# Forgetting attention with a gated layer on one core: seven-product second layers moved from units 1-7 to units 2-8, weight sums cut into 16 pieces, transposes of results issued earlier

## The chip, the cores and the metric

The kernel runs on one core of one Trainium2 chip. The metric is the device time of the core in microseconds (us). A profile shows one execution; its span is the stretch from the first to the last recorded event, and its own time is a little longer than the span.

Engines are called as in the profile: PE (TensorE, matrix products), PEld (loading of PE's weights), DVE (VectorE), ACT (ScalarE), POOL (GpSimd) and SP (SyncE, here a queue of transfers).

## The reference

```python
batch, n_heads, seq, head_dim = (8, 8, 576, 64)      # q, k, v; f is (8, 8, 576)
d_model, d_ff = (512, 2048)

def _attn_ref(q, k, v, f):
    scores = scale * np.matmul(q, k.transpose(0, 1, 3, 2))
    cum = np.cumsum(np.log(np.clip(f, 0.0001, 1.0)), axis=-1)
    decay = cum[:, :, :, None] - cum[:, :, None, :]
    scores = np.where(causal, -1000000000.0, scores + decay)
    attn = np.exp(scores - np.max(scores, axis=-1, keepdims=True))
    attn = attn / (np.sum(attn, axis=-1, keepdims=True) + 1e-09)
    return np.matmul(attn, v)

x = attn_out.transpose(0, 2, 1, 3).reshape(4608, 512)
h = x @ w_in
out = (h - np.tanh(h)) @ w_out
```

So there is causal attention with a decay for 64 heads of 576 positions, and then two dense layers (512 to 2048 to 512) with a gate between them, on 4608 tokens.

## The kernel before, in words

**Attention** goes by pairs of heads: eight batches of four pairs, 32 pairs in all. A pair has seven score tiles (`scores`, `TILES`); each is two or so matmuls on PE, an exponential on ACT and, from batch 2 on, a mask on POOL. `values` multiplies the exponentials with v (30 small matmuls into `av`), and DVE norms the result into `xn`. `turn` then has SP transpose `xn` by two transfers into `XR`, a ring of three batches that holds the tokens as columns for the first layer. `values` and `turn` of a pair run in the slot of the following pair.

**The dense layers** go by nine units of 512 tokens (`UW`). `mlp1` is the first layer: 16 steps, each with four matmuls of 512 columns into a bank `hps`, a tanh on ACT and an addition on DVE (`gate`) which leaves a gated tile in 16 bits. The second layer has two forms:

- plain (`mlp2`): 16 steps of four matmuls of 512 columns.
- seven products (`seven`): the second layer is taken as a product of 2 x 2 blocks, and seven block products replace eight. A unit has 14 steps of eight matmuls of 256 columns (seven products, two halves `m` each). For this DVE forms four sums of the gated tile's quarters in each of four tiles (`sums`, L421), and once for the whole kernel sums of the second weight (`weight_sums`, L429): `t1`, `t2`, `t3`, `tn4`. They lie in the buffers that held q and k of batch 3 (`qn`, `kn` in the profile) and in `tn4`. The products gather in two banks, `cx` and `cz`; ACT copies `cx` out (L507, L515, L518, L523), DVE adds `cz` (L486), and four stores on SP (L483) write the result. Products 2 and 4 start `cz` afresh, products 3, 5 and 6 go on in `cx`.

`fast(u)` says which units use seven products: units 1 to 7. Units 0 and 8 are plain. The last block of rows of unit 8 is done by `last_rows` in two column parts.

**The order is written by hand** for all five engines. The list `mlp` holds all 274 steps of the dense layers in order. There are 33 slots of attention: those of the first batch are written out, and `slot(p, take)` runs from p = 4 to 32. It goes through the items of a pair (score tiles s0 to s6, turning of q and k for batches 1 and 2, `values`, `turn`, and the loads of `LOADS`) and puts `take` dense steps between them, evenly. `TAKE` has the counts. What is left of the steps, those of units 7 and 8, runs after the last slot: the tail, with no attention beside it.

`LOADS` hangs other work on a slot's score tile: loads of later batches (POOL), transposes of q and k (SP), their placing (`place`, L106, eight DVE copies in every fourth slot from p = 11 on) and the weight sums (p = 10).

Each engine does its instructions in the order in which they are written, and so does each queue of transfers. SP carries the transposes of `xn` and the stores of results in one queue.

The lines that fix a product's bank, and the sums that follow it:

```python
        ps = (x, x, z, z, x, x, z, z, x, x, x, x, z, z)[s]
        fresh = ph in (0, 1, 3)
```

Of the kernel before, what the change touches and what calls it, by code (L numbers as in the profile page):

```python
# [22 lines left out]
def kernel(  # L23
# [10 lines left out]
    nc = tc.nc  # L34
# [169 lines left out]
    def load_qk(dst, src, b, h0, h1):  # L204
# [3 lines left out]

    LOADS = {(NPAIR, 5): [lambda: load_qk(qn, q, 2, 0, H)],
             (NPAIR, 6): [lambda: load_qk(kn, k, 2, 0, H)]}  # L210
    for i, ti in enumerate((1, 2, 4, 5)):
        LOADS.setdefault((2 * NPAIR + 2, ti), []).append(lambda i=i: weight_sums(i))
    for b in range(2, B):
        p0 = (b - 1) * NPAIR
        for n in range(NJ):
# [191 lines left out]
        nc.vector.tensor_tensor(out=to, in0=view(hps), in1=view(th), op=ALU.add)  # L407

    def fast(u):
        return 0 < u < NU - 1  # L410

    def quarter(u, k, hf, e):
        return G[(u, k)].rearrange("p (h e) n -> p h e n", h=2)[:, hf, e, :]
# [7 lines left out]
        nc.vector.tensor_tensor(out=out, in0=in0, in1=in1, op=op)  # L421

    def weight_sums(i):
        b11, b12 = wout[:, 0:HF, 0:HD], wout[:, 0:HF, HD:DM]
        b21, b22 = wout[:, HF:NFT, 0:HD], wout[:, HF:NFT, HD:DM]
        for out, in0, in1 in ([(t1, b12, b11)], [(t3, b22, b12)],
                              [(t2[x], b22[:, 4 * x:4 * x + 4, :], t1[:, 4 * x:4 * x + 4, :]) for x in range(2)],
                              [(tn4[:, 4 * x:4 * x + 4, :], b21[:, 4 * x:4 * x + 4, :], t2[x]) for x in range(2)])[i]:
            nc.vector.tensor_tensor(out=out, in0=in0, in1=in1, op=ALU.subtract)  # L429

    def mlp1(u, s):
        hps = ps_m.tile([P, UW], FP32, tag="m", name="hps")
        gt = gate_tile(u, s)
        if u == 0:
            t, fp = s // 4 % 2, s // 8 * 4 + s % 4
            for w in range(2):
                ft = 2 * fp + w
                for ci in range(NCH):
                    nc.tensor.matmul(out=hps[:, w * SB:(w + 1) * SB], lhsT=win[:, ci, ft * P:(ft + 1) * P],  # L439
                                     rhs=XR[:, ci, t * SB:(t + 1) * SB], start=(ci == 0), stop=(ci == NCH - 1))  # L440
            gate(hps, gt[:, s % 4, :])
            for w in range(2):
                for m in range(2):
                    GT[(0, 2 * fp + w, 2 * t + m)] = gt[:, s % 4, w * SB + m * P:w * SB + (m + 1) * P]
            return
        ft = s // 4 * 2 + s % 4 // 2 + HF * (s % 2) if fast(u) else s
        t0 = u * UW % RING
        parts = [(0, t0, min(UW, RING - t0))]
        if t0 + UW > RING:
            parts.append((RING - t0, 0, t0 + UW - RING))  # L450
        for o, t, n in parts:
            for ci in range(NCH):
                nc.tensor.matmul(out=hps[:, o:o + n], lhsT=win[:, ci, ft * P:(ft + 1) * P],  # L453
                                 rhs=XR[:, ci, t:t + n], start=(ci == 0), stop=(ci == NCH - 1))
# [10 lines left out]
    CH = {}  # L465

    def stationary(u, what, ft, m):
        k, at = ft // 2, slice(ft % 2 * SB + m * P, ft % 2 * SB + (m + 1) * P)
# [9 lines left out]
            return t2[ft // 4][:, ft % 4, :]  # L478
        return {"t1": t1, "t3": t3, "tn4": tn4}[what][:, ft, :]

    def store(u, e, d, src):
        rows = out[u * UW:(u + 1) * UW, d * HD:(d + 1) * HD].rearrange("(m p e) c -> e p m c", p=P, e=2)
        nc.sync.dma_start(out=rows[e], in_=src.rearrange("p (m c) -> p m c", m=2))  # L483

    def add(to, ps):
        nc.vector.tensor_tensor(out=to, in0=ps, in1=to, op=ALU.add)  # L486

    def seven(u, s):
        ph, m = divmod(s, 2)
        if s == 0:  # L490
            CH["x"] = ps_m.tile([P, UW], FP32, tag="m", name="cx")
            for i in range(3):
                sums(u, HF // 2 - 1, i)
# [3 lines left out]
        ps = (x, x, z, z, x, x, z, z, x, x, x, x, z, z)[s]  # L497
        fresh = ph in (0, 1, 3)
        lhs, rhs = ("a11", "a12", "s2", "s1", "s3", "a22", "s4")[ph], ("b11", "b21", "t2", "t1", "t3", "tn4", "b22")[ph]
        for ft in range(HF):  # L500
            nc.tensor.matmul(out=ps[:, m * SB:(m + 1) * SB], lhsT=stationary(u, lhs, ft, m), rhs=moving(rhs, ft),  # L501
                             start=fresh and m == 0 and ft == 0, stop=(ft == HF - 1), skip_group_check=True)
        if m == 0:
            return
        if ph == 0:
            CH["p1"] = snap[0][:, 0:UW]
            nc.scalar.activation(out=CH["p1"], in_=x, func=AF.Copy)  # L507
        if ph == 1:
            add(CH["p1"], z)
            store(u, 0, 0, CH["p1"])  # L510
            for k in range(HF // 2):
                sums(u, k, 3)
        if ph == 2:
            CH["u2"] = snap[1][:, 0:UW]
            nc.scalar.activation(out=CH["u2"], in_=x, func=AF.Copy)  # L515
        if ph == 4:
            u3 = tmp.tile([P, DM], FP32, tag="ost", name="u3")
            nc.scalar.activation(out=u3, in_=x, func=AF.Copy)  # L518
            add(u3, z)
            store(u, 1, 1, u3)  # L520
        if ph == 5:
            ost = tmp.tile([P, DM], FP32, tag="ost", name="ost")
            nc.scalar.activation(out=ost, in_=x, func=AF.Copy)  # L523
            store(u, 1, 0, ost)
        if ph == 6:
            add(CH["u2"], z)
            store(u, 0, 1, CH["u2"])

    def last_rows(u, m):
        r0 = u * UW + m * P  # L530
        for c0, c1 in ((0, 3 * P), (3 * P, DM)):
            ops = ps_m.tile([P, DM], FP32, tag="m", name="ops")[:, 0:c1 - c0]
            for ft in range(NFT):
                nc.tensor.matmul(out=ops, lhsT=GT[(u, ft, m)], rhs=wout[:, ft, c0:c1],  # L534
                                 start=(ft == 0), stop=(ft == NFT - 1))
            ost = tmp.tile([P, DM], FP32, tag="ost", name="ost")[:, 0:c1 - c0]
            nc.vector.tensor_copy(out=ost, in_=ops)
            nc.sync.dma_start(out=out[r0:r0 + P, c0:c1], in_=ost)

    def mlp2(u, s):  # L540
        m, part = divmod(s, 4)
        if u == NU - 1 and m == UW // P - 1:
            if part == 0:
                last_rows(u, m)
            return
        if part == 0:
            M2[u] = ps_m.tile([P, DM], FP32, tag="m", name="ops")
        ops = M2[u]
# [8 lines left out]

    pairs = [(b, c) for b in range(B) for c in range(NPAIR)]

    mlp = [(fn, 0, s) for fn in (mlp1, mlp2) for s in range(NFT)]  # L560
    for u in range(1, NU - 1):
        ahead = 2 * (u == NU - 2)
        mlp += [(mlp1, u, s) for s in range(NFT)]
        mlp += [(seven, u, s) for s in range(10)]
        mlp += [(mlp1, u + 1, s) for s in range(ahead)]
        mlp += [(seven, u, s) for s in range(10, 14)]
    mlp += [(mlp1, NU - 1, s) for s in range(2, NFT)]
    mlp += [(mlp2, NU - 1, s) for s in range(NFT)]
    done = [0]

    def step(n=1):
# [6 lines left out]
    def att_items(p):  # L578
# [16 lines left out]
        return items  # L595

    def slot(p, take):
        items = att_items(p)
        whole, n, given = sum(c != "" for _, c in items), 0, 0
        for i, (emit, what) in enumerate(items):  # L600
            emit()
            if take in FEW:
# [4 lines left out]
            while (given + 1) * whole <= n * take:  # L607
                step()
                given += 1
        if take not in FEW:  # L610
            step(take - given)

    load_v(0, 0)
    spin(6)
# [134 lines left out]
```

## Time and profile before

| | us |
|---|---|
| median of three runs | 365.15 (363.15 to 365.9) |
| the profiled execution, its own time | 362.69 |
| its span | 361.0 |
| PE busy | 337.7 (94%) |
| DVE busy | 249.7 (69%) |
| ACT busy | 221.1 (61%) |
| POOL busy | 156.1 (43%) |

The share of PE is an average over stages, and its matmuls are pipelined with modelled ends. So the places where PE waits are read from the windows, the waits and the chain, and a wait counts where PE is the engine that sets the pace.

### The profile page before, as it was taken

What the parts mean: (1) busy time and instruction counts of PE and PEld (TensorE: products, weight loads), DVE (VectorE), ACT (ScalarE), POOL (GpSimd) and SP (SyncE); (2) the same over time, 40 slices, a digit from 0 to 9 for tenths busy, and PEclk for the clock granted to TensorE, in tenths of its full rate; (3) what the DMA queues carried; (4) which work ended last, traced back from release to release, by engine and by line L of the source; (5) the groups of instructions that cost most, each with busy time, mean ns of one, the idle gap of its engine ahead of it and who ended that gap; (6) DMA issues with size and microseconds to landing.
All of it is one profiled execution on the core that took longest, in us unless ns stands there. A gap on an engine that the chain in (4) does not pass through costs nothing.

```text
span 361.0 us, 8828 instructions
## 1 busy us (share of the span) xinstructions
PE 337.7 (94%) x3400; PEld 236.2 (65%) x3400; DVE 249.7 (69%) x503; ACT 221.1 (61%) x413; POOL 156.1 (43%) x291
## 2 busy tenths in 40 slices
PE   6889999999587999999999999999999996999996
PEld 3778875555266657788876577657777883477443
DVE  6588886369995499648964896489548832973720
ACT  5678885456543787578657865786578621633720
POOL 8974424563355545854585459542322210000000
PEclk9999999999999999999999999999999998999999
DMA  9999999999098995999799999991231012002002
GB/s 87 144 206 183 206 182 157 146 211 103 16 70 94 175 143 64 135 167 140 82 125 163 161 69 125 156 170 40 64 98 21 19 56 80 0 32 71 17 29 88
DMA packets 152172, 38.76 MB, mean 107 GB/s; under 512 B 137346, under 2 KB 150210, under 8 KB 152130
## 3 DMA queue, kind: packets, MB, share of 16 engines
q0 software_dynamic: 100128, 18.36, 70.5%
q1 hardware_dynamic: 51922, 19.78, 30.7%
q8 instruction: 26, 0.43, 0.5%
q14 instruction: 16, 0.13, 0.2%
q10 hardware_dynamic: 80, 0.07, 0.1%
HBM read 36.85 MB, written 9.44 MB: 128 GB/s over the span
## 4 chain that ended last, share of the span: by engine, by line
PE 75%; DMA 9%; DVE 8%; ACT 3%; issue 2%; POOL 1%; SPq 1%; DVEq 0%; POOLq 0%; ACTq 0%
PE hps L453 27%; PE cx L501 13%; PE cz L501 10%; PE ps L350 8%; DMA kn<-in_k_dram 7%; PE ops L550 6%; PE av L378 6%; DVE gt L407 2%; DMA TK<-kn 1%; ACT e L297 1%; ACT u L518 1%; PE ops L534 1%; PE ps L292 1%; PE hps L439 1%; PE t L264 1%
## 5 line engine op out<-in xcount | busy, mean ns | idle before, releaser
L453 PE MATMUL hps<-XR,win 128*128 128x512 f16 (+4 forms) x640 | 127.6, 339 | 7.4 <-DVE gt L407 4.2
L359 ACT ACTIVATE e<-ps 128x512 f16<-128x512 f32 x168 | 98.4, 594 | 43.4 <-PE ps L350 38.4
L407 DVE TENSOR_TENSOR gt<-hps,th 128x512 f16<-128x512 f32 x144 | 98.9, 688 | 27.8 <-ACT th L406 26.8
L406 ACT ACTIVATE th<-hps 128x512 f32<-128x512 f32 x144 | 86.1, 598 | 43.8 <-PE hps L453 30.2
L369 POOL TENSOR_SCALAR_AFFINE_SELECT e<-e 128x128 f16<-128x128 f16 x144 | 53.6, 374 | 103.2 <-ACT e L359 102.5
L453 PEld LDWEIGHTS <-win 128*128 128x128 f16 x640 | 56.7, 98 | 52.2 <-issue 10.6
L350 PE MATMUL ps<-QT,KT 67*128 67x512 f16 (+1 forms) x336 | 69.5, 277 | 0.2 <-ACT e L359 0.2
L501 PEld LDWEIGHTS <-gt 128*128 128x128 f16 x560 | 52.4, 97 | 13.4 <-issue 4.8
L350 PEld LDWEIGHTS <-KT 67*128 67x128 f16 x336 | 32.3, 98 | 19.0 <-issue 0.5
L94 POOL DMA_DIRECT2D vn<-in_v_dram x40 | 34.1, 857 | 10.2 <-PE ps L350 3.6
L378 PEld LDWEIGHTS <-e 128*128 128x128 f16 x784 | 28.0, 97 | 2.8
L378 PE MATMUL av<-vn,e 128*128 128x65 f16 x784 | 29.2, 193 | 0.0
L501 PE MATMUL cz<-wout,gt 128*128 128x256 f16 x224 | 28.0, 272 | 0.0
L486 DVE TENSOR_TENSOR snap<-cz,snap 128x512 f32<-128x512 f32 x14 | 9.6, 686 | 25.7 <-PE cz L501 24.8
L550 PE MATMUL ops<-wout,gt 128*128 128x512 f16 x112 | 26.8, 379 | 0.0
L94 POOL DMA_DIRECT2D qn<-in_q_dram x25 | 21.2, 849 | 10.0 <-DMA wout<-in_moe_w_out_dram 3.9
L501 PEld LDWEIGHTS <-sw 128*128 128x128 f16 x224 | 20.8, 97 | 6.7 <-issue 1.6
L386 DVE TENSOR_TENSOR xn<-av,rs 128x640 f16<-128x640 f32 x28 | 23.1, 825 | 1.0
L94 POOL DMA_DIRECT2D kn<-in_k_dram x25 | 21.3, 853 | 1.4 <-issue 1.2
L501 PE MATMUL cx<-tn,gt 128*128 128x256 f16 x112 | 14.2, 272 | 3.8 <-ACT u L518 3.8
L297 ACT ACTIVATE e<-ps 128x512 f16<-128x512 f32 x25 | 14.2, 596 | 4.8 <-PE ps L295 3.0
L550 PEld LDWEIGHTS <-gt 128*128 128x128 f16 x112 | 10.2, 97 | 10.4
(108 smaller groups left out, 397.0 us busy)
## 6 DMA issues: line engine op xcount, KB each, us to landing
vn<-in_v_dram POOLq DMA_DIRECT2D x32, 128.0 KB, 5.5
out_dram<-ost SPq DMA_DIRECT2D x14, 256.0 KB
out_dram<-snap SPq DMA_DIRECT2D x14, 256.0 KB
qn<-in_q_dram POOLq DMA_DIRECT2D x24, 128.0 KB, 3.7
kn<-in_k_dram POOLq DMA_DIRECT2D x24, 128.0 KB, 4.7
win<-in_moe_w_in_dram POOLq DMA_DIRECT2D x2, 1024.0 KB, 11.4
wout<-in_moe_w_out_dram POOLq DMA_DIRECT2D x4, 512.0 KB, 12.0
out_dram<-u SPq DMA_DIRECT2D x7, 256.0 KB
```

Of the source, the lines that this page charges most:

```text
L94: nc.gpsimd.dma_start(out=dst[0:pn, n, h0:h1, 0:D], in_=src[b, h0:h1, n * P:n * P + pn, :].rearrange("h p d -> p h d"))
L297: nc.scalar.activation(out=e, in_=ps, func=AF.Exp, scale=qscale)
L350: nc.tensor.matmul(out=ps[:, col:col + n], lhsT=KT[b % 2][0:D + 3, h, j * P:(j + 1) * P], rhs=QT[b % 2][0:D + 3, h, i0:i0 + n], start=True ...
L359: nc.scalar.activation(out=e[:, lo:hi], in_=ps[:, lo:hi], func=AF.Exp, scale=qscale)
L369: nc.gpsimd.affine_select(out=view, in_=view, compare_op=ALU.is_ge, fill=0.0, base=0, pattern=pat, channel_multiplier=-1)
L378: nc.tensor.matmul(out=av[:, a, ib, :], lhsT=E.pop((b, 2 * c + a, j, ib)), rhs=vn[b % 2][:, j, 2 * c + a, 0:D + 1], start=(j == 0), stop=( ...
L386: nc.vector.tensor_tensor(out=xn.rearrange("p i (a d) -> p a i d", a=2), in0=av[:, :, :, 0:D], in1=rs.to_broadcast([P, 2, NJ, D]), op=ALU. ...
L406: nc.scalar.activation(out=th, in_=hps, func=AF.Tanh, scale=-1.0)
L407: nc.vector.tensor_tensor(out=to, in0=view(hps), in1=view(th), op=ALU.add)
L453: nc.tensor.matmul(out=hps[:, o:o + n], lhsT=win[:, ci, ft * P:(ft + 1) * P], rhs=XR[:, ci, t:t + n], start=(ci == 0), stop=(ci == NCH - 1))
L501: nc.tensor.matmul(out=ps[:, m * SB:(m + 1) * SB], lhsT=stationary(u, lhs, ft, m), rhs=moving(rhs, ft), start=fresh and m == 0 and ft == 0 ...
L550: nc.tensor.matmul(out=ops, lhsT=GT[(u, ft, m)], rhs=wout[:, ft, :], start=(ft == 0), stop=(ft == NFT - 1))
```

## The change

1. `fast(u)` becomes `u > 1`: units 0 and 1 are plain, units 2 to 8 use seven products.
2. Unit 8 gets a form of its own, `last_seven`: the two halves `m` of the `cx` chain have banks of their own (`x`, `y`), the seventh product a bank `w`, and the order of the last two products is exchanged. `last_rows` is gone.
3. The weight sums come in 16 pieces of two weight tiles (512 elements a partition), four to a slot, in slots 11 to 14.
4. Of the four sums of a gated tile the first two follow the gates; the third follows steps 1 and 3 of the products and the fourth steps 5 and 7 (`more_sums`).
5. The first step of the sixth product (step 10) is held back until two attention items have been written since the step before it; what is owed is then made up (`held`, `upto`, `goal`).
6. `turn` follows `values` directly; before, the dense steps due after `values` were written between them.
7. `TAKE` for slots 10 to 16 goes from 8, 8, 8, 8, 8, 7, 7 to seven times 8 (its entries from p = 10 on).

The diff, cut to its core:

```diff
-    for i, ti in enumerate((1, 2, 4, 5)):
-        LOADS.setdefault((2 * NPAIR + 2, ti), []).append(lambda i=i: weight_sums(i))
+    for i in range(2 * HF):
+        LOADS.setdefault((2 * NPAIR + 3 + i // 4, i % 4 * 2), []).append(lambda i=i: weight_sums(i))
...
     def fast(u):
-        return 0 < u < NU - 1
+        return u > 1
...
     def weight_sums(i):
...
+        what, x = divmod(i, HF // 2)
+        lo, hi = slice(2 * x, 2 * x + 2), slice(HF + 2 * x, HF + 2 * x + 2)
...
-        if s > 3 and s % 4 < 3:
+        if s > 3 and s % 4 < 2:
             sums(u, s // 4 - 1, s % 4)
...
+    def more_sums(u, s):
+        k = HF // 2 - 1
+        if s == 0:
+            sums(u, k, 0)
+            sums(u, k, 1)
+        if s in (1, 3):
+            sums(u, s - 1, 2)
+            sums(u, s, 2)
+        if s in (5, 7):
+            sums(u, s - 5, 3)
+            sums(u, s - 4, 3)
...
+    def last_seven(u, s):
+        if s == 0:
+            for n in "xy":
+                CH[n] = ps_m.tile([P, UW], FP32, tag="m", name="c" + n)
+            CH["z"] = ps_tr.tile([P, UW], FP32, tag="tr", name="cz")
+            CH["w"] = ps_m.tile([P, UW], FP32, tag="m", name="cw")
+        ph, m = divmod(s, 2)
+        ph = (0, 1, 2, 3, 4, 6, 5)[ph]
+        at = slice(m * SB, (m + 1) * SB)
+        z, w = CH["z"], CH["w"]
+        chain = CH["xy"[m]][:, 0:SB]
+        if ph in (1, 3, 6):
+            product(u, ph, m, (w if ph == 6 else z)[:, at], m == 0)
+        else:
+            product(u, ph, m, chain, ph == 0)
...
+        if ph == 5:
+            ost = tmp.tile([P, DM], FP32, tag="ost", name="ost")[:, 0:SB]
+            if m:
+                nc.vector.tensor_copy(out=ost, in_=chain)
+            else:
+                nc.scalar.activation(out=ost, in_=chain, func=AF.Copy)
+            store(u, 1, 0, ost, m, m + 1)
+        more_sums(u, s)
...
             if ti == 1 and before:
-                items.append((lambda: values(*before), "v"))
-                items.append((lambda: turn(*before), ""))
+                items.append((lambda: (values(*before), turn(*before)), "v"))
...
+    def held():
+        fn, _, s = mlp[done[0]]
+        return fn is seven and s == 10 and since[0] < 2
+
+    def upto(n):
+        while done[0] < n and not held():
+            step()
+            since[0] = 0
...
-    TAKE = [4, 4, 4, 3, 10, 9, 8, 8, 8, 8, 8, 7, 7] + 4 * [8, 7, 8, 7]
+    TAKE = [4, 4, 4, 3, 10, 9] + 7 * [8] + 4 * [8, 7, 8, 7]
```

More of the change, by code (lines that the diff above doesn't have):

```diff
@@ L423, in weight_sums @@
     def weight_sums(i):
[L424 to L429, printed above, removed]
+        what, x = divmod(i, HF // 2)
+        lo, hi = slice(2 * x, 2 * x + 2), slice(HF + 2 * x, HF + 2 * x + 2)
+        b11, b12, b21, b22 = (wout[:, r, c] for r in (lo, hi) for c in (slice(0, HD), slice(HD, DM)))
+        t2x = t2[x // 2][:, x % 2 * 2:x % 2 * 2 + 2, :]
+        out, in0, in1 = ((t1[:, lo, :], b12, b11), (t2x, b22, t1[:, lo, :]),
+                         (t3[:, lo, :], b22, b12), (tn4[:, lo, :], b21, t2x))[what]
+        nc.vector.tensor_tensor(out=out, in0=in0, in1=in1, op=ALU.subtract)
     def mlp1(u, s):
@@ L479, in moving, with store, product @@
         return {"t1": t1, "t3": t3, "tn4": tn4}[what][:, ft, :]
-    def store(u, e, d, src):
+    def store(u, e, d, src, m0=0, m1=2):
         rows = out[u * UW:(u + 1) * UW, d * HD:(d + 1) * HD].rearrange("(m p e) c -> e p m c", p=P, e=2)
-        nc.sync.dma_start(out=rows[e], in_=src.rearrange("p (m c) -> p m c", m=2))
+        nc.sync.dma_start(out=rows[e][:, m0:m1, :], in_=src.rearrange("p (m c) -> p m c", c=HD))
     def add(to, ps):
         nc.vector.tensor_tensor(out=to, in0=ps, in1=to, op=ALU.add)
+    LHS = ("a11", "a12", "s2", "s1", "s3", "a22", "s4")
+    RHS = ("b11", "b21", "t2", "t1", "t3", "tn4", "b22")
+    def product(u, ph, m, ps, fresh):
+        for ft in range(HF):
+            nc.tensor.matmul(out=ps, lhsT=stationary(u, LHS[ph], ft, m), rhs=moving(RHS[ph], ft),
+                             start=fresh and ft == 0, stop=(ft == HF - 1), skip_group_check=True)
+    def more_sums(u, s):
[9 more added lines that the diff above has]
+            sums(u, s - 4, 3)
     def seven(u, s):
         ph, m = divmod(s, 2)
+        at = slice(m * SB, (m + 1) * SB)
         if s == 0:
             CH["x"] = ps_m.tile([P, UW], FP32, tag="m", name="cx")
-            for i in range(3):
-                sums(u, HF // 2 - 1, i)
         if s == 2:
@@ L496, in seven @@
         x, z = CH["x"], CH.get("z")
[L497 to L502, printed above, removed]
@@ L503, in seven @@
-        if m == 0:
-            return
-        if ph == 0:
[L506 to L512, printed above, removed]
+        product(u, ph, m, (z if ph in (1, 3, 6) else x)[:, at], ph in (0, 1, 3) and m == 0)
+        if m:
+            if ph == 0:
+                nc.scalar.activation(out=P1, in_=x, func=AF.Copy)
+            if ph == 1:
+                add(P1, z)
+                store(u, 0, 0, P1)
+            if ph == 2:
+                nc.scalar.activation(out=U2, in_=x, func=AF.Copy)
+            if ph == 4:
+                u3 = tmp.tile([P, DM], FP32, tag="ost", name="u3")
+                nc.scalar.activation(out=u3, in_=x, func=AF.Copy)
+                add(u3, z)
+                store(u, 1, 1, u3)
+            if ph == 5:
+                ost = tmp.tile([P, DM], FP32, tag="ost", name="ost")
+                nc.scalar.activation(out=ost, in_=x, func=AF.Copy)
+                store(u, 1, 0, ost)
+            if ph == 6:
+                add(U2, z)
+                store(u, 0, 1, U2)
@@ new lines, in seven @@
+        more_sums(u, s)
[7 more added lines that the diff above has]
+        ph = (0, 1, 2, 3, 4, 6, 5)[ph]
+        at = slice(m * SB, (m + 1) * SB)
+        z, w = CH["z"], CH["w"]
[4 more added lines that the diff above has]
+            product(u, ph, m, chain, ph == 0)
+        if ph == 0:
+            nc.scalar.activation(out=P1[:, at], in_=chain, func=AF.Copy)
+        if ph == 1 and m:
+            add(P1, z)
+            store(u, 0, 0, P1)
@@ L513, in seven @@
         if ph == 2:
-            CH["u2"] = snap[1][:, 0:UW]
-            nc.scalar.activation(out=CH["u2"], in_=x, func=AF.Copy)
+            nc.scalar.activation(out=U2[:, at], in_=chain, func=AF.Copy)
+        if ph == 3 and m:
+            CH["u3"] = tmp.tile([P, DM], FP32, tag="ost", name="u3")
         if ph == 4:
[L517 to L520, printed above, removed]
@@ L521, in seven @@
-        if ph == 5:
[L522 to L538, printed above, removed]
+            nc.scalar.activation(out=CH["u3"][:, at], in_=chain, func=AF.Copy)
@@ new lines, in last_seven @@
+            if m:
+                add(CH["u3"], z)
+                add(U2, z)
+                store(u, 1, 1, CH["u3"])
+        if ph == 6 and m:
+            add(U2, w)
+            store(u, 0, 1, U2)
+        if ph == 5:
+            ost = tmp.tile([P, DM], FP32, tag="ost", name="ost")[:, 0:SB]
+            if m:
+                nc.vector.tensor_copy(out=ost, in_=chain)
+            else:
+                nc.scalar.activation(out=ost, in_=chain, func=AF.Copy)
+            store(u, 1, 0, ost, m, m + 1)
@@ L540, in mlp2 @@
+        more_sums(u, s)
     def mlp2(u, s):
         m, part = divmod(s, 4)
[L542 to L545, printed above, removed]
         if part == 0:
@@ L558 @@
     pairs = [(b, c) for b in range(B) for c in range(NPAIR)]
[L560 to L563, printed above, removed]
+    mlp = [(fn, u, s) for u in range(2) for fn in (mlp1, mlp2) for s in range(NFT)]
+    for u in range(2, NU):
+        late = 2 * (u == NU - 1)
+        mlp += [(mlp1, u, s) for s in range(late, NFT)]
+        if u == NU - 1:
+            mlp += [(last_seven, u, s) for s in range(14)]
+            continue
         mlp += [(seven, u, s) for s in range(10)]
-        mlp += [(mlp1, u + 1, s) for s in range(ahead)]
+        mlp += [(mlp1, u + 1, s) for s in range(2 * (u == NU - 2))]
         mlp += [(seven, u, s) for s in range(10, 14)]
-    mlp += [(mlp1, NU - 1, s) for s in range(2, NFT)]
-    mlp += [(mlp2, NU - 1, s) for s in range(NFT)]
     done = [0]
@@ L595, in att_items @@
         return items
+    goal, since = [0], [0]
+    def held():
[5 more added lines that the diff above has]
+            since[0] = 0
     def slot(p, take):
         items = att_items(p)
-        whole, n, given = sum(c != "" for _, c in items), 0, 0
+        whole, n, base = sum(c != "" for _, c in items), 0, goal[0]
         for i, (emit, what) in enumerate(items):
             emit()
-            if take in FEW:
+            since[0] += what != ""
+            if take in FEW and p < 2 * NPAIR:
                 if what in FEW[take] and not (what == "s1" and p > NPAIR) or what == "v":
@@ L606, in slot @@
             n += what != ""
[L607 to L611, printed above, removed]
+            upto(base + n * take // whole)
+        goal[0] = base + take
+        upto(goal[0])
     load_v(0, 0)
```

2 lines of the change are left out of this document (added).

## The prediction

> **What bounds the kernel now.** I read the table of windows first, cut where the stages change, because the page's 94% PE hides where the idle time lies. Columns: stretch, length, busy time (count) of PE, PEld, DVE, ACT, POOL, then granted clock, DMA share, GB/s.
>
> ```profile
> 85.00:110.00 25.00, 18.44 (x172) 11.69 (x171) 24.66 (x46) 13.18 (x26) 10.58 (x19) 1.00 0.62 54
> 110.00:119.00 9.00, 8.38 (x98) 7.22 (x98) 3.12 (x8) 3.64 (x7) 5.42 (x10) 1.00 0.95 102
> 119.00:158.00 39.00, 38.38 (x372) 26.62 (x370) 28.29 (x57) 27.28 (x52) 23.82 (x47) 1.00 1.39 137
> 158.00:293.00 135.00, 133.13 (x1428) 98.84 (x1426) 101.79 (x210) 94.16 (x181) 66.33 (x139) 1.00 1.01 102
> 293.00:303.00 10.00, 6.28 (x54) 5.05 (x52) 1.98 (x3) 1.19 (x2) 0.00 (x0) 0.98 0.31 94
> ```
>
> PE sets the pace almost everywhere: it idles 0.62 us of 39 and 1.87 of 135. Two holes stand out. In 85 to 110 PE lacks 6.56 us while DVE is full (24.66 of 25). In 293 to 303 it lacks 3.72 us and every engine is idle. The list of waits names what ends the idle time (total us, times, longest):
>
> ```profile
> PE hps L453 <- DVE gt L407: 4.2, 3, 2.3
> PE cx L501 <- ACT u L518: 3.8, 6, 0.7
> PE hps L453 <- DMA XR<-xn: 3.0, 1, 3.0
> PE cz L501 <- DVE snap L486: 1.3, 1, 1.3
> ```
>
> So there are three kinds: DVE late with gates (and once with the add that frees cz), a 0.62 to 0.68 us wait in every unit of seven products, and one DMA wait. The chain that ended last (start, us, what) shows the DMA wait and the end:
>
> ```profile
> 293.16 1.76 PE cx L501 x16
> 294.94 0.60 ACT u L518
> ...
> 297.49 1.76 PE cz L501 x16
> 299.28 0.70 DVE snap L486
> 300.46 2.42 DMA XR<-xn
> 302.93 14.91 PE hps L453 x61
> ...
> 331.89 12.09 PE hps L453 x56
> 343.98 10.36 PE ops L550 x48
> 354.34 3.51 PE ops L534 x32
> 357.93 0.29 DVE ost L537
> ```
>
> The last transposes of XR stand on SP's queue behind the store of the seventh product's result, which waits for the add at 299.28. After 302.93 PE runs without a gap to 357.85.
>
> Unit prices: a plain step (4 matmuls of 512) is 10.36/48 x 4 = 0.863 us; a product step (8 of 256) is 1.76/2 = 0.88. A plain second layer costs 16 x 0.863 = 13.8 us, seven products 14 x 0.88 = 12.3.
>
> **The change, part by part.**
>
> *Which steps lie where.* By the step lists both versions have 274 steps. Before, unit 1 holds steps 32 to 61; after, 32 to 63, so unit 2 starts at 64. The new counts per slot (8, 8 in place of the last 7, 7) put unit 2 at the same slots, 13 to 16, and all later units with it. The tail still begins with unit 7. So each unit meets the same attention work as before.
>
> *Early stage: the weight sums and unit 1's sums go.* In 85 to 110 the groups of DVE are:
>
> ```profile
> L407 DVE TENSOR_TENSOR gt<-hps,th 128x512 f16<-128x512 f32 x10 | 6.8, 683 | 0.1
> L421 DVE TENSOR_TENSOR gt<-gt 128x512 f16<-128x512 f16 x4 | 1.8, 449 | 0.0
> L421 DVE TENSOR_TENSOR sw<-gt 128x512 f16<-128x512 f16 x3 | 1.3, 440 | 0.0
> L421 DVE TENSOR_TENSOR sw<-sw,gt 128x512 f16<-128x512 f16 x3 | 1.3, 418 | 0.0
> L429 DVE TENSOR_TENSOR kn<-wout 128x2048 f16<-128x2048 f16 x1 | 1.2, 1219 | 0.0
> L429 DVE TENSOR_TENSOR kn<-wout,qn 128x1024 f16<-128x1024 f16 x1 | 0.9, 884 | 0.0
> L429 DVE TENSOR_TENSOR tn<-wout,qn 128x1024 f16<-128x1024 f16 x1 | 0.7, 682 | 0.0
> ```
>
> With a second of 1.22 and two more of 0.68, the weight sums take 5.4 us here. Unit 1's sums take 4.4 in these rows, one more sum and the add 1.1. So near 10.8 of 24.66 leave. A new piece of 512 elements has the size of the L421 rows, 0.43 us; four (1.7) come into slot 11, the other twelve go to slots 12 to 14. DVE is then at 15.6 us against 18.44 of PE, so PE is the bound again. In slot 10 alone (eight gates of 0.69, two copies of KT, a norm) DVE still nearly equals PE, so I leave 0.5 of the idle time. The wait of 0.62 in 110 to 119 goes with unit 1's sixth product. **Gain 6.56 + 0.62 - 0.5 = 6.7**; bounds: 4.2 (only the named waits on gates) and 7.2 (all).
>
> *Unit 1 plain.* PE is the bound there, so it costs **13.8 - 12.3 = +1.5**.
>
> *The pieces in slots 12 to 14.* Slot 14 has eight gates, four sums, four pieces and a norm: with the 0.61 that gates take back to back (start to start) some 9.3 us, against 9.2 on PE: 8 x 0.863 and 2.3 of attention (the values 0.90, six score tiles of 0.22, one tiny, from the rows of the next part but one). It comes out even; with the three buffers of hps I take 0, at most 1.
>
> *Sums regrouped.* Two of four sums now come with the gates, the third with steps 0 to 3 of the products, the fourth with steps 5 and 7. What matters is DVE's queue ahead of the add that frees cz. One unit, before (DVE's timeline, start and length, and PE's row for cz):
>
> ```profile
> 176.06 1.00 DVE L106 COPY QT<-TQ 64x1152 f16<-64x1152 f16 x2
> 176.99 0.41 DVE L421 TENSOR_TENSOR sw<-gt 128x512 f16<-128x512 f16 x1
> 177.43 0.42 DVE L421 TENSOR_TENSOR sw<-sw,gt 128x512 f16<-128x512 f16 x1
> 177.77 0.42 DVE L421 TENSOR_TENSOR gt<-gt 128x512 f16<-128x512 f16 x1
> ...
> 180.96 0.67 DVE L486 TENSOR_TENSOR snap<-cz,snap 128x512 f32<-128x512 f32 x1
> ...
> 181.93 1.04 PE L501 MATMUL cz<-qn,sw 128*128 128x256 f16 x8
> ```
>
> DVE runs without a gap to the add, which ends at 181.63; PE overwrites cz at 181.93, so 0.3 us is spare. Afterwards four sums instead of three stand ahead of it: 0.35 to 0.42 later, so the overwrite waits about 0.1. In unit 2, shifted by one step, a gate more (0.69) stands ahead: about 0.4. With unit 2 at 0.4 and units 3 to 6 at 0.1, **+0.8**; bounds 0 and +3 (0.6 each).
>
> *Sixth product held.* It waits for ACT's copy of cx (a piece of the chain, then PE's timeline):
>
> ```profile
> 148.11 0.90 PE av L378 x30
> ...
> 150.81 0.23 PE L350 MATMUL ps<-QT,KT 67*128 67x64 f16 x2
> 151.66 1.03 PE L501 MATMUL cx<-tn,gt 128*128 128x256 f16 x8 [0.62 <-ACT u L518]
> 152.53 0.38 PE L350 MATMUL ps<-QT,KT 67*128 67x512 f16 x1
> ```
>
> Before, only the tiny tile of 64 columns stands between. After, the next score tile (152.53 to the next step at 152.75, so 0.22 us) moves ahead of the product. What queues behind the held step are the product's own later steps, which follow two at a time; PE does the same work. The gain is 0.22 in units 2 to 5: **-0.9**; bounds 0 and 4 x 0.62 = 2.5. In slot 32 there is only one item, so unit 6 keeps its 0.68.
>
> *Results turned sooner.* The last xn is ready early:
>
> ```profile
> 292.77 0.82 DVE L386 TENSOR_TENSOR xn<-av,rs 128x640 f16<-128x640 f32 x1
> ```
>
> Its two transposes now enter SP's queue before the stores of that slot. Issued at 293.6 and taking 2.42, they land at 296.1, before PE wants them at 299.1. **The whole 3.04 goes.** The stores behind them start at 296.3 and later anyway; in other slots SP waits for xn a little ahead of stores whose buffers are wanted a unit later. The stall also cost clock:
>
> ```profile
> 303.00:305.00 2.00, 2.00 (x5) 0.62 (x5) 0.69 (x1) 0.60 (x1) 0.00 (x0) 0.50 0.04 7
> 305.00:307.00 2.00, 2.00 (x8) 0.83 (x7) 0.69 (x1) 1.00 (x2) 0.00 (x0) 0.74 0.00 0
> 307.00:309.00 2.00, 2.00 (x11) 0.90 (x10) 1.43 (x3) 1.39 (x3) 0.00 (x0) 1.00 0.00 0
> ```
>
> 61 matmuls took 14.91 where 61 x 12.09/56 = 13.17 would do: 1.74 lost. Clocks of 0.50 and 0.74 over two 2-us stretches explain 1.0 + 0.5. I take **1.6 back**; bounds 0 and 1.74.
>
> [...] The rows show 0.50 straight after the gap; the measurement decides.
>
> *Last unit in seven products.* PE needs 12.3 where the chain has 10.36 + 3.51 = 13.87. The first product reads gates of the last steps 0.76 us after its start, where a plain step had 2.6; I put 0.2 for that. The split banks let ACT copy one half while PE fills the other, so no further waits inside. **-1.35**; bounds -1.6 and 0 (should the first product have to wait for the last gate, 1.4).
>
> *The end.* The last copy is 256 columns instead of 128, the last store 128 KB instead of 64, and a 256 KB store goes out just before. Copy 0.29 to some 0.42, and a little more DMA: **+0.3**; bounds 0 and +1.1.
>
> **Sum:** -6.7 + 1.5 + 0.8 - 0.9 - 3.04 - 1.6 - 1.35 + 0.3 = -11.0. The profiled execution took 362.69 us (span 361.0, 1.7 around it); it becomes 351.7. That execution lies 2.5 below the median 365.15, so against the median I forecast 365.15 - 11.0 = **354.1**. Its own range, with some bounds on either side at once, is 350 to 358.
>
> **The rivals.**
>
> *A: DVE becomes the bound around the products.* For it: DVE runs gapless up to the add, and 16 pieces cost more than the undivided sums (16 x 0.43 = 6.9 against 5.4). Against it: 101.79 of 135 us busy. If the add comes 0.9 late in units 2 to 6, that is 4.5 instead of 0.8: 354.1 + 3.7 = 357.8.
>
> *B: the turn doesn't do what it says.* If the last transposes still land late, behind another store or a slow DMA, 4.64 stays: 358.7. For it: SP's queue is in order. Against it: no store of that slot is now ahead, and the landing has 3 us to spare.
>
> *C: slower.* The place is cz alone: held steps come two at a time and the sums stand denser, so the add is late in all of units 2 to 6 and PE waits each time. Price: 5 x 3.1 us = 15.5 less the 0.8 counted, 368.8. It turns the result from (11.0 + 0.8)/5 = 2.4 us per unit on. For it: only 0.3 us spare today. Against it: one sum more ahead of the add is 0.4 us; six would be needed.
>
> *D: the clock isn't given back.* What lost 1.6 us after the gap was no consequence of the gap: 355.7. Against it stand the rows of clock above. [...]
>
> **How the numbers follow.** Forecast 0.69, A 0.13, B 0.08, C 0.07, D 0.03. About 1% (3.65 us) is what a measurement can tell here. Forecast, A, B and D all lie over 1% below 365.15 (under 361.5), but for some 0.04 of their bad ends. C is split around its edge, 0.02 within 1% and 0.05 beyond. Hence faster 0.89, same 0.06, slower 0.05. The range from 350.0 to 359.5 covers the forecast's own bounds and A, B and D at their prices.
>
> **What would show it.** Right: no wait of PE for DVE gates near 85 to 110; no wait of PE for XR near 299 and a clock of 1.00 throughout the tail; three to four waits of cx for ACT's copy near 0.4 and one of 0.68; the last PE stage near 12.4 us. Wrong: PE waiting for the add on cz by 0.5 us or more in each unit (A, C), a DMA wait for XR (B), or DVE full in slots 12 to 15. If the span is not below 356, one of the two big terms, the early DVE stall or the turn, has failed.

## The result, and the profile after

The changed kernel takes 353.39 us (median of four runs, 352.57 to 354.65) against 365.04: a ratio of 0.9691 with a 95% interval of 0.964 to 0.9742. The forecast was 354.1. The profiled execution has a span of 350.9 where the one before had 361.0, so 10.1 us are to be explained.

The windows of the changed kernel, cut at its own stages, with the columns of the windows shown before:

```profile
85.00:110.00 25.00, 24.90 (x214) 13.40 (x212) 21.72 (x41) 15.99 (x31) 13.54 (x27) 1.00 1.08 92
110.00:119.00 9.00, 9.00 (x75) 4.79 (x74) 2.72 (x6) 6.00 (x13) 5.89 (x11) 1.00 1.67 160
119.00:154.00 35.00, 33.39 (x333) 23.60 (x331) 27.23 (x58) 23.83 (x46) 19.55 (x39) 1.00 1.09 118
154.00:289.00 135.00, 132.75 (x1411) 98.03 (x1408) 101.48 (x207) 93.24 (x180) 64.99 (x139) 1.00 0.93 101
289.00:295.00 6.00, 5.32 (x50) 4.61 (x49) 1.99 (x4) 1.19 (x2) 0.00 (x0) 1.00 0.25 68
```

Both holes are closed: PE is busy 24.90 of 25 us in 85 to 110, and there is no 3 us gap near 295. The waits of PE from 85 us on (total, times, longest) are down to two:

```profile
PE cx L495 <- ACT u L529: 2.3, 5, 0.7
PE cz L495 <- DVE snap L488: 2.2, 3, 1.2
```

The chain that ended last, in the tail:

```profile
290.97 0.60 ACT u L529
291.62 1.91 PE cx L495 x16
293.52 1.75 PE cz L495 x16
295.27 13.81 PE hps L454 x64
...
323.14 12.09 PE hps L454 x56
335.23 0.97 PE cx L495 x8
...
346.68 0.89 PE cy L495 x8
347.57 0.02 issue
347.59 0.42 DVE ost L577
```

Unit 7's first layer follows the last product directly, 64 matmuls in 13.81 us with the clock at 1.00. The last second layer runs from 335.23 to 347.57.

To see where the 10.1 us came from, I use the starts of `values` on PE as milestones: slots 10, 17 and 32. The first three rows are the kernel before, the others the changed one (PE's timeline):

```profile
85.46 0.58 PE L378 MATMUL av<-vn,e 128*128 128x65 f16 x14
158.00 0.59 PE L378 MATMUL av<-vn,e 128*128 128x65 f16 x14
291.09 0.58 PE L378 MATMUL av<-vn,e 128*128 128x65 f16 x14
86.37 0.58 PE L378 MATMUL av<-vn,e 128*128 128x65 f16 x14
153.39 0.59 PE L378 MATMUL av<-vn,e 128*128 128x65 f16 x14
287.11 0.58 PE L378 MATMUL av<-vn,e 128*128 128x65 f16 x14
```

| stretch | before | after | difference | forecast |
|---|---|---|---|---|
| start to slot 10 | 85.46 | 86.37 | +0.91 | 0 |
| slot 10 to 17 (weight sums, units 1 and 2) | 72.54 | 67.02 | -5.52 | -5.0 |
| slot 17 to 32 (units 3 to 6) | 133.09 | 133.72 | +0.63 | -0.3 |
| slot 32 to the end | 69.91 | 63.79 | -6.12 | -5.7 |

The forecast column adds up the prediction's terms by place. In the first stretch PE does the same 971 matmuls in both kernels. In all thirteen profiles of this study it lies between 85.2 and 87.8, with values on both sides of the 85.46 of before among the kernels that hold the change. So I don't count the +0.91 as the change's, and much of the spread of a kernel's runs may come from there; with one profile a kernel that is not shown.

One of the four executions of b_unit1, a kernel of the next section, was in a slower state (364.25 us, mean clock 0.981) and is left out of its median.

### The profile page after: what moved, and what is told of

Read it like the earlier page. It is cut to its first block, busy times and chain, and to the rows that moved or that the text cites. A ratio compares the mean times of both kernels' runs of the same rounds, so it can differ in the third digit from the quotient of the medians.

```text
span 350.9 us, 8809 instructions
## 1 busy us (share of the span) xinstructions
PE 338.0 (96%) x3384; PEld 237.5 (68%) x3384; DVE 251.7 (72%) x513; ACT 222.5 (63%) x417; POOL 153.5 (44%) x291
## 4 chain that ended last, share of the span: by engine, by line
PE 88%; DVE 6%; ACT 4%; issue 1%; DMA 1%; ACTq 0%; DVEq 0%
PE hps L454 30%; PE cx L495 12%; PE cz L495 10%; PE ps L350 10%; PE ops L589 8%; PE av L378 7%; PE hps L440 3%; PE ps L292 2%; PE t L264 1%; DVE KT L106 1%; ACT e L297 1%; PE cy L495 1%; DVE gt L407 1%; ACT u L529 1%; PE t L246 1%
## 5 line engine op out<-in xcount | busy, mean ns | idle before, releaser
L454 PE MATMUL hps<-XR,win 128*128 128x512 f16 (+4 forms) x640 | 125.9, 336 | 0.2
L369 POOL TENSOR_SCALAR_AFFINE_SELECT e<-e 128x128 f16<-128x128 f16 x144 | 51.3, 357 | 99.9 <-ACT e L359 97.7
L495 PEld LDWEIGHTS <-gt 128*128 128x128 f16 x560 | 52.8, 97 | 11.6 <-issue 3.6
L589 PE MATMUL ops<-wout,gt 128*128 128x512 f16 x128 | 32.5, 378 | 0.0
L495 PE MATMUL cz<-wout,gt 128*128 128x256 f16 x208 | 25.9, 272 | 0.0
L589 PEld LDWEIGHTS <-gt 128*128 128x128 f16 x128 | 11.0, 97 | 10.1
L440 PE MATMUL hps<-XR,win 128*128 128x256 f16 x128 | 16.6, 272 | 0.0
```

Of the source, the lines that this page charges most:

```text
L369: nc.gpsimd.affine_select(out=view, in_=view, compare_op=ALU.is_ge, fill=0.0, base=0, pattern=pat, channel_multiplier=-1)
L495: nc.tensor.matmul(out=ps, lhsT=stationary(u, LHS[ph], ft, m), rhs=moving(RHS[ph], ft), start=fresh and ft == 0, stop=(ft == HF - 1), skip ...
```

## The experiments

The milestones of every profiled run are used, because they leave out the unsteady start (us; "10-17" is slot 10 to slot 17, and so on). The kernels were timed in four groups, each beside the kernel before, whose median was 365.04, 363.44, 363.89 and 363.79 us. So medians of different groups can't be compared to 1 or 2 us; the ratio to before in the same group can, within its interval of about 0.004 to either side (0.003 to 0.008).

| kernel | median time | ratio to before | 10-17 | 17-32 | 32-end |
|---|---|---|---|---|---|
| before | 365.04 | 1 | 72.54 | 133.09 | 69.91 |
| after | 353.39 | 0.9691 | 67.02 | 133.72 | 63.79 |
| turn_late | 353.26 | 0.9725 | 67.00 | 133.71 | 65.27 |
| both_late | 357.96 | 0.9862 | 67.22 | 134.37 | 66.93 |
| nohold | 353.24 | 0.9723 | 67.22 | 134.38 | 63.70 |
| plain8 | 353.58 | 0.9733 | 67.00 | 133.71 | 64.92 |
| sums12 | 353.60 | 0.9757 | 67.00 | 133.71 | 63.95 |
| b_nosums | 359.89 | 0.9874 | 68.14 | 133.08 | 68.19 |
| b_unit1 | 360.77 | 0.9899 | 69.30 | 133.08 | 69.90 |
| addfirst | 350.81 | 0.9634 | 66.45 | 132.42 | 63.78 |
| swap | 350.51 | 0.9644 | 66.45 | 132.06 | 62.87 |
| swap_add | 347.62 | 0.9570 | 65.88 | 130.74 | 62.87 |
| swap_add_place | 346.81 | 0.9543 | 65.08 | 130.75 | 62.89 |

### The early hole: weight sums or unit 1's sums?

b_nosums is the kernel before without weight sums:

```diff
+        what = {"t1": "b11", "t3": "b12", "t2": "b22", "tn4": "b21"}.get(what, what)
         if what[0] == "b":
...
-    for i, ti in enumerate((1, 2, 4, 5)):
-        LOADS.setdefault((2 * NPAIR + 2, ti), []).append(lambda i=i: weight_sums(i))
```

> The kernel before without its weight sums; products that use t1, t2, t3 and tn4 read blocks of the second weight instead, so PE does the same work and the output isn't the reference's. Theory (the weight sums and unit 1's own sums together fill DVE): 5.4 of 24.7 us leave DVE in 85 to 110, PE's idle time there falls from 6.6 to 1 to 2 us, and the time falls by 5, to 360. Rival (the idle time came from the wait for the transposes of K, or from unit 1's sums): it falls by less than 2.

b_unit1 is the kernel before with unit 1 plain:

```diff
-        return 0 < u < NU - 1
+        return 1 < u < NU - 1
...
-    TAKE = [4, 4, 4, 3, 10, 9, 8, 8, 8, 8, 8, 7, 7] + 4 * [8, 7, 8, 7]
+    TAKE = [4, 4, 4, 3, 10, 9] + 7 * [8] + 4 * [8, 7, 8, 7]
```

> The kernel before with unit 1 plain (seven products for units 2 to 7 only) and the step counts of the changed kernel; the weight sums stay undivided in slot 10. Theory: unit 1's sums (5.5 us) leave DVE in 85 to 110, PE's idle time there falls from 6.6 to 1 to 3 us, PE's work grows by 1.5, and the 0.62 of unit 1's sixth product goes: the time falls by 3 to 5, to 360 to 362. Rival (the undivided weight sums alone are the stall): idle time stays at 4 us or more and the time falls by less than 2.

The first row is b_nosums in the early stretch, the second b_unit1:

```profile
85.00:110.00 25.00, 22.18 (x232) 15.27 (x230) 22.79 (x48) 14.45 (x28) 11.53 (x23) 1.00 0.75 74
85.00:110.00 25.00, 22.78 (x199) 12.24 (x197) 21.01 (x38) 15.04 (x29) 12.43 (x24) 1.00 0.93 69
```

PE's idle time there falls from 6.56 to 2.8 us without the weight sums, where 1 to 2 was expected, and to 2.2 with unit 1 plain, as expected. Slots 10 to 17 shorten by 4.40 and by 3.24 us (the latter with 1.5 us more work for PE in it). The ratios are 0.9874 (0.9817 to 0.9932) and 0.9899 (0.9829 to 0.997). So both rivals fall: each of the two piles on DVE had to be there to make the hole, and taking away either removes more than half of it. They don't add up: 3.7 and 4.4 us of idle time went, and only 6.5 with both, in the changed kernel.

sums12 puts the weight sums undivided into slot 12 of the changed kernel:

```diff
-    for i in range(2 * HF):
-        LOADS.setdefault((2 * NPAIR + 3 + i // 4, i % 4 * 2), []).append(lambda i=i: weight_sums(i))
+    for i, ti in enumerate((1, 2, 4, 5)):
+        LOADS.setdefault((3 * NPAIR, ti), []).append(lambda i=i: weight_sums(i))
```

> The changed kernel with the weight sums undivided as before, in slot 12 (score tiles 1, 2, 4, 5), in which the dense steps are all of unit 1's plain second layer. Theory (what helped was that the sums moved to slots where DVE has nothing urgent, not that they were cut): no new wait of PE near 105 to 115, and with nothing left in slots 13 and 14 unit 2's wait for the add on cz shrinks from 1.20 to 0.8 or less; time 353.4 or up to 0.6 less. Rival (small pieces are what keeps PE running): PE waits 1 to 4 us more between 100 and 135, time 355 to 357.

PE's windows from 100 to 135, the changed kernel first, then sums12:

```profile
100.00:135.00 35.00, 35.00 (x292) 19.07 (x290) 26.06 (x53) 24.76 (x46) 21.66 (x42) 1.00 1.30 127
100.00:135.00 35.00, 35.00 (x281) 18.46 (x280) 25.35 (x46) 25.47 (x48) 21.75 (x41) 1.00 1.24 130
```

No new wait, and slots 10 to 17 take the same 67.0. The cutting into 16 pieces is worth nothing here; the move is what counts. (This rests on the profile: one of the four times of sums12 was 357.46, and the time alone leaves it open.) My own side expectation fell as well: unit 2's wait for cz stayed at 1.2, so the pieces in slots 13 and 14 were not its cause.

### The gap before unit 7: the turn, the hold and the clock

turn_late:

```diff
-                items.append((lambda: (values(*before), turn(*before)), "v"))
+                items.append((lambda: values(*before), "v"))
+                items.append((lambda: turn(*before), ""))
```

> The changed kernel with turn put back behind the dense steps that are due after values. Theory (the wait and the clock both follow from the late turn): PE waits some 3 us for XR at the end of unit 6, the clock falls to near 0.5 after it, and unit 7's first 61 matmuls take 1.5 to 1.7 us more than 13.2; the time rises by 4.6, from 353.4 to 358. Rival (the 1.7 us came from the denser sums on DVE, which the change thinned out): the wait comes back, the slow stretch doesn't, and the time rises by 3.0 to 356.4. Second rival (the transposes would have landed in time anyway): no change.

Neither the theory nor the rivals had this. The chain of turn_late:

```profile
291.63 1.16 PE cx L495 x10
292.80 4.42 DMA XR<-xn
297.22 0.04 issue
297.26 13.32 PE hps L454 x61
```

PE waited 1.3 us for XR, not 3, and the clock stayed at 1.00 (in the windows from 296 to 302). The reason is in the hold. In slot 32 there is one attention item, so step 10 of unit 6 is held, and only steps 7 to 9 stand between `values` and `turn`. So SP has one store (of u3) ahead of the transposes, not three (SP's queue):

```profile
292.33 0.37 SPq L485 DMA_DIRECT2D out_dram<-u  x1
292.80 1.23 SPq L393 DMA_TRANSPOSE XR<-xn  x1
```

The hold brings the last transposes forward as well. Slot 32 to the end grew by 1.5 us; the time (ratio to before 0.9725, 0.9685 to 0.9766, against 0.9691 for the changed kernel) can't tell it.

nohold:

```diff
-        return fn is seven and s == 10 and since[0] < 2
+        return False
```

> The changed kernel with the sixth product never held. Theory: the wait of cx for ACT's copy is 0.62 instead of 0.41 in units 2 to 5 and the rest stays: the waits of cx in all go from 2.3 to about 3.1 us, the time rises by 0.8 at most, not told apart from 353.4 by the time alone. Rival (holding back makes steps come in twos and costs elsewhere): the time falls, or the waits of cz for the add shrink from 2.2 us.

The waits of PE in nohold:

```profile
PE cx L495 <- ACT u L529: 3.2, 5, 0.7
PE cz L495 <- DVE snap L488: 2.2, 3, 1.2
```

As the theory had it: 0.62 instead of 0.41 in four units, 0.2 and 0.66 us in the two stretches, and nothing in the tail, where the turn alone is enough. The waits of cz don't move.

both_late has both edits.

> The changed kernel with turn behind the dense steps again and nothing held, so that all seven steps of the last slot stand between values and turn, as before the change. Theory (in the last slot the hold and the earlier turn overlap: either brings the last transposes ahead of most stores): PE waits 3.0 to 3.1 us for XR, where turn alone put back gave 1.3; with a clock that stays at 1.00 the time rises by 0.9 (no hold) and 3.0 to 357.2, with a clock that falls to 0.5 by 1.6 more, to 358.8. Rival (the changed stores and sums around it, not hold and turn, brought XR forward): a wait of 1.3 us or less.

```profile
PE hps L454 <- DMA XR<-xn: 3.0, 1, 3.0
```

Now the full 3.0 us are back (waits of PE in both_late), and from slot 10 to the end it takes 4.0 us more than the changed kernel: 0.85 without the hold, as in nohold, and 3.1 in the tail. The ratio, 0.9862, is clear of 0.9691. So hold and turn overlap, and either alone removes 1.7 us or more of the gap.

What the gap does to the clock differs from run to run. The rows are two windows after the gap: of both_late, of b_nosums and of b_unit1, whose waits for XR were 3.0, 3.1 and 3.1 us:

```profile
302.00:304.00 2.00, 2.00 (x11) 0.93 (x10) 1.66 (x3) 1.27 (x3) 0.00 (x0) 1.00 0.00 0
300.00:302.00 2.00, 2.00 (x11) 0.88 (x9) 1.32 (x2) 1.47 (x3) 0.00 (x0) 1.00 0.01 0
302.00:304.00 2.00, 2.00 (x7) 0.62 (x6) 1.38 (x2) 0.67 (x2) 0.00 (x0) 0.50 0.00 0
```

The 61 matmuls after the gap take, from the chains of the same three:

```profile
300.92 13.33 PE hps L454 x61
299.47 13.38 PE hps L451 x61
301.06 15.07 PE hps L453 x61
```

The clock (last but two in a window's row) fell in two of four profiled executions with such a gap (the kernel before and b_unit1) and not in the other two. In none of the nine other profiles, in which the gap is 1.3 us or gone, does it fall there (a matmul of unit 7's first layer takes 0.216 us in all nine, as in the 12.09 us for 56 matmuls at a clock of 1.00). It also settles what the lost time is. b_nosums has the same dense sums on DVE in unit 7 as the kernel before, and its 61 matmuls take 13.38: the sums cost nothing there, the clock costs 1.5 to 1.7 (14.91 and 15.07 against 13.33 and 13.38).

### Unit 8 in seven products

plain8 makes unit 8 plain again, with `last_rows`:

```diff
-        return u > 1
+        return 1 < u < NU - 1
...
-            mlp += [(last_seven, u, s) for s in range(14)]
+            mlp += [(mlp2, u, s) for s in range(NFT)]
```

> The changed kernel with unit 8 plain again, its last rows in two column parts as before. Theory: the last stage of PE takes 13.87 us instead of about 12.5, the end after PE's last matmul is 0.2 us shorter; the time rises by 1.2, to 354.6. Rival (the last store of 128 KB behind one of 256 KB eats the gain): PE ends 1.4 us later but the span grows by less than 0.5.

The end of its chain:

```profile
334.49 10.36 PE ops L604 x48
344.85 3.51 PE ops L588 x32
...
348.43 0.29 DVE ost L591
```

From the first matmul of the last second layer PE needs 13.87 us, where the changed kernel needs 12.34; slot 32 to the end is 1.13 us longer. The end after PE's last matmul is 0.36 us longer with the larger last store (3.31 against 2.95), more than the 0.2 expected, and does not eat the gain. The time can't tell a change of this size (ratio 0.9733, 0.9695 to 0.9772, against 0.9691).

### What is left: two waits, and a better version

addfirst:

```diff
-        if s in (1, 3):
-            sums(u, s - 1, 2)
-            sums(u, s, 2)
-        if s in (5, 7):
-            sums(u, s - 5, 3)
-            sums(u, s - 4, 3)
+        if s in (4, 5):
+            sums(u, 2 * s - 8, 2)
+            sums(u, 2 * s - 7, 2)
+        if s in (6, 7):
+            sums(u, 2 * s - 12, 3)
+            sums(u, 2 * s - 11, 3)
```

> The changed kernel with the third sum moved from steps 1 and 3 to steps 4 and 5 and the fourth from 5 and 7 to 6 and 7, so that only two sums stand on DVE ahead of the add that frees cz. Theory (the sums ahead of the add are why cz waits): the add comes 0.75 us earlier, the waits of cz fall from 2.2 us (1.20, 0.37, 0.66) to about 0.5 (only unit 2's), the time falls by 1.5 to 1.9, to 351.7. Rival (the copies of L106 and the norm are what makes DVE late, and what is moved comes in the way later): the waits of cz stay above 1.5, or s3 and s4 become late.

Its waits of PE from 85 us on:

```profile
PE cx L495 <- ACT u L529: 2.3, 5, 0.7
PE cz L495 <- DVE snap L488: 0.6, 1, 0.6
```

The waits of cz fall from 2.2 to 0.6 and the time to 350.81 (ratio to before 0.9634, 0.9596 to 0.9672). Two sums fewer ahead of the add are enough to end the waits of units 3 and 4 and to halve that of unit 2; what else made the add late there is told below.

swap exchanges the last two products in all units, as unit 8 already has them. The seventh goes to a bank of its own, and z is added to both results:

```diff
+        ph = (0, 1, 2, 3, 4, 6, 5)[ph]
...
+        if s == 10:
+            CH["w"] = ps_m.tile([P, UW], FP32, tag="m", name="cw")
...
-        return fn is seven and s == 10 and since[0] < 2
+        return False
...
-        mlp += [(mlp1, u + 1, s) for s in range(2 * (u == NU - 2))]
```

> The changed kernel with the last two products exchanged in all units (seventh into a bank of its own before the sixth), nothing held back and no steps of unit 8 drawn ahead. Theory: ACT's copy of cx has two product steps of 0.88 to hide behind, so the waits of cx for it (2.3 us: 0.41 four times, 0.69) go; one more add of 0.6 in each unit on DVE does not show; the time falls by 2.0 to 2.3, to 351.3. Rival (the extra bank taken from the three of hps makes the next unit's first layer wait, or the added DVE work delays the next gates): new waits of hps for gates of 0.3 us or more a unit, time 353 or more.

The waits of cx are gone and no new one came. The time is 350.51 (0.9644, 0.9578 to 0.9709). From slot 10 on swap is 3.1 us shorter than the changed kernel, more than the 2.0 to 2.3 expected and than the 2.33 of listed waits that went. The reason lies in how a wait is listed. A product step's row lasts 1.03 to 1.04 us, but steps that don't wait start 0.87 to 0.88 apart: the modelled end of a row lies some 0.16 us behind the moment at which the next step could start, and a listed wait counts only from that end. So I estimate a wait that goes altogether at its listed length and 0.16 more, here 2.33 + 5 x 0.16 = 3.1.

swap_add has both edits.

> The changed kernel with the last two products exchanged in all units and with the third and fourth sums behind the add that frees cz. Theory (the two waits are separate and add up): the waits of cx for ACT go, those of cz fall to 0.6, and the gains of the two single edits (2.6 and 2.9 us) add up to some 5: time 348.2. Rival (with one wait gone DVE's queue makes another): cz waits 1.5 us or more again, or hps waits for gates; time 350 or more.

They add up: from slot 10 on addfirst is 1.9 us shorter than the changed kernel, swap 3.1, swap_add 5.0; the time is 347.62 (0.957, 0.954 to 0.960). PE's only wait from 85 us to the end is

```profile
PE cz L495 <- DVE snap L488: 0.6, 1, 0.6
```

swap_add_place moves the placing of K behind the add:

```diff
-                    LOADS.setdefault((p0 + 3, 2 * n + a), []).append(...)
+                    LOADS.setdefault((p0 + 3, 4 * n + a), []).append(...)
```

> As the kernel with both edits, and in addition the four copies that place K of the next batch (L106) moved from score tiles 2 and 3 to 4 and 5 of their slot. Theory (the copies ahead of the add are what is left of unit 2's wait for cz): the last 0.6 us goes, time 0.6 lower, 347.6. Rival: the next slot's first score tile waits for KT by 0.5 us or more in some of five slots, and the time is the same or higher.

Two windows of it:

```profile
110.00:154.00 44.00, 44.00 (x436) 30.50 (x435) 32.94 (x70) 30.92 (x59) 26.16 (x52) 1.00 1.36 131
154.00:283.00 129.00, 129.00 (x1370) 95.45 (x1369) 100.49 (x205) 91.63 (x176) 62.48 (x135) 1.00 0.93 103
```

PE has no gap left in the slots. The time is 346.81 (0.9543, 0.9508 to 0.9579); slots 10 to 17 are 0.8 us shorter than in swap_add, the last 0.6 and the 0.16 of above, while the medians of the last two kernels are too close to be told apart by time. Either beats both kernels of this case.

## Why the prediction was right

**The sum.** -11.0 was forecast and the medians moved by 11.65; the profiled spans moved by 10.1, and by 11.0 without the start, which was 0.91 slower. That the sum fits so closely is partly luck. By the milestones, with 0.16 added for each wait that went or came, the early hole gave about 1.5 us more than forecast and the waits of cz cost about 1.9 more; the other terms were each right to 0.2 and make up the rest.

**The early hole.** The step held: DVE's load fell below PE's and PE became the bound, with an idle time of 0.1 us in 85 to 110 (0.5 was allowed for). But the term was too small. Slots 10 to 17 shrank by 5.5 although unit 1's plain layer cost 1.5 there and unit 2's wait for cz 1.4, with 0.2 won by the hold: so the early hole gave about 8.2, where 6.7 was forecast and 7.2 was the upper bound. The step that failed is "7.2 (all)": it took the idle time of the windows for all that a wait costs. Seven waits went, six of them in 85 to 110, and 7 x 0.16 = 1.1 is the difference to the listed 7.1. The experiments add that the two things removed from DVE do not add up. The pieces in slots 12 to 14 cost PE nothing, as forecast: it is busy 35.00 of 35 us in 100 to 135.

**Sums regrouped.** This term was mis-sized. It was put at 0.4 for unit 2 and 0.1 for units 3 to 6, 0.8 in all; it measured 1.20, 0.37 and 0.66 in units 2 to 4 and nothing in units 5 and 6, 2.2 in all, or 2.7 with 0.16 for each wait. DVE and PE in unit 2 and in unit 3, and DVE in unit 5, which doesn't wait, from the timelines after:

```profile
137.86 0.84 DVE L421 TENSOR_TENSOR gt<-gt 128x512 f16<-128x512 f16 x2
138.62 2.18 DVE L106 COPY KT<-TK 64x1152 f16<-64x1152 f16 x4
140.83 0.69 DVE L488 TENSOR_TENSOR snap<-cz,snap 128x512 f32<-128x512 f32 x1
141.58 1.03 PE L495 MATMUL cz<-qn,sw 128*128 128x256 f16 x8 [1.20 <-DVE snap L488]
175.87 1.34 DVE L106 COPY KT<-TK 64x1152 f16<-64x1152 f16 x2
177.84 1.03 PE L495 MATMUL cz<-qn,sw 128*128 128x256 f16 x8 [0.37 <-DVE snap L488]
248.69 0.91 DVE L106 COPY KT<-TK 64x1152 f16<-64x1152 f16 x2
```

The prediction counted one 512-element sum more ahead of the add. In unit 2 the shift by one step also puts all four copies of KT ahead of it (2.18 us in a row), where unit 3 has two there. That second effect of the shift was left out: the copies' place among the steps. In units 3 and 4 the two copies ahead of the add also took some 0.4 us longer than in unit 5 or, in the kernel before, in unit 3 (1.34 and 1.26 against 0.91), for which the prediction had no term; I come back to it at the end. swap_add_place, which moves them behind the add, removes the 0.6 that addfirst leaves of unit 2's wait.

**The hold.** The 0.21 per unit (0.62 to 0.41) is as forecast, and unit 6 kept its 0.69.

**The turn.** The gap of 3.04 went, as forecast, but its attribution failed at one step. "In slot 32 there is only one item, so unit 6 keeps its 0.68" was followed only as far as PE's wait. The same hold also takes the late stores off SP's queue ahead of the transposes, so the hold alone would have left only 1.3 of the 3.04.

**The clock.** 1.6 was forecast as given back, and that is its size: 14.91 against the 13.32 to 13.38 which the same 61 matmuls take behind a gap with the clock at 1.00. (Without a gap they take 13.16, 61/64 of 13.81, which is 0.16 less again.) But it is no fixed price: such a gap lowered the clock in two of four executions, and the 61 matmuls took 14.91 and 15.07 there and 13.33 and 13.38 in the other two. What decides between the two outcomes no run shows.

**The last unit.** 12.5 us were forecast for its products with 0.2 of wait, 12.34 measured, and the end grew by 0.2 over the kernel before, as against 0.3.

**The rivals.** A (DVE becomes the bound around the products) was the direction in which the forecast erred, 1.4 us of listed waits where it would have cost 3.7. B didn't happen, and C's mechanism exists at a tenth of its price. D did not come true, since the time was given back with the gap. What speaks against it is that the low clock stands behind a gap of 3 us in two of four profiles and in that place in none of the nine others; b_nosums shows only that the gap doesn't always cost it and that the dense sums are not the reason.

## What to carry to other kernels

Where two engines are nearly level, ask of each added operation which waiting instruction it stands ahead of on its in-order queue, not how busy the engine is: taking two small sums of each unit (0.75 us) from ahead of one add was worth 1.9 us in all by the milestones, cutting the weight sums into 16 pieces nothing. When a result is waited for, exchange it with work that needs nothing new (here the last two products) before holding it back. And when an edit delays steps, follow it into every queue that those steps feed: the hold, meant for PE, also brought a transfer on SP forward (PE's wait for XR was 1.3 us in turn_late, which has the hold, and 3.0 in both_late, which has not).

## What the hardware showed that I had not expected

A gap of 3.0 to 3.1 us on PE lowers the granted clock to 0.5 for some 3 us (0.50 from 303 to 306 in the kernel before; 0.50 and then 0.65 in the two windows from 302 to 306 of b_unit1) in some executions and not in others of nearly the same program (two of four here), which is a spread of up to 1.7 us from the clock alone. A gap of 1.3 us did not lower it in the one profile that has it (turn_late, 1.00 from 296 to 302).

The same copy on DVE (L106, 64 x 1152 in 16 bits) takes 0.44 to 0.46 us in all 132 cases of the thirteen profiles in which POOL neither masks scores nor issues a load beside it, and 0.44 to 0.90 in the 388 in which it does; those of 0.86 and more ahead of the add in units 3 and 4 stand beside a load's issue. That POOL's work is the cause fits this, but no run varied it alone.
